# A seven-matmul prelude, exponentials on either of two engines, and wider staging in a fused attention, expert-attention and MLP kernel

## The chip, the cores and the metric

The kernel runs on one core of one Trainium2 chip. The metric is the device time of one execution in microseconds; a kernel's time is the median of several runs.

## What is computed

Three layers follow one another on data of 4 batches and 576 positions.

```
scores = 0.125 * q @ k.T          # 4 batches, 8 heads, 576 positions, width 64
# heads 0 to 3: key in the last 32 positions; heads 4 to 7: every 4th of the last 128
attn = softmax(where(mask, scores, -1e9)) @ v           # -> x, [4, 576, 512]
...
# 4 experts e, causal attention of width 64 each, the best 2 of 4 weighted per position
a = softmax(causal(0.125 * (x @ wq[e]) @ (x @ wk[e]).T))
x = sum over chosen e of w[e] * (a @ (x @ wv[e]) @ wo[e])
...
xn = (x - mean) / sqrt(var + 1e-6) * g_ln
out = x + relu(xn @ w_ch1) @ w_ch2                      # 512 -> 2048 -> 512
```

## The kernel before

**Stages.** Each batch goes through the windowed attention by pairs of heads (four pairs, written (b, hp); pairs 0 and 1 have the plain window, 2 and 3 the dilated one), then through projections for the experts, causal attention by tiles of 128 queries, and an output projection. All 2304 positions then go through the MLP, which is 1,824 wide matmuls and fills the time from about 320 us on. Products that need more than one pass of the fast number format are made of three matmuls of high and low parts.

**Order.** The order of the instructions on every engine is written by a planner in the kernel (`run_chains`). Each piece of work is a generator ("chain") that yields operations with an engine, an estimated duration and the times at which its inputs are ready. The planner always takes the operation that can start first, and so fixes each engine's program order from estimated times. An engine works through its own list strictly in that order: an instruction that waits holds up what stands behind it. Where a chain yields `either(...)`, the planner picks the engine that could start the operation first. The estimates are in `landing` (when a load is there), in `act` and `dve` (durations by elements) and in the numbers at each `op`.

**Loads.** All loads go through SyncE's queue (SP). `all_loads` lists them in a fixed order: per batch and pair q and k (`load_qk`), then v (`load_v`), with the weights in between. q and k land in two staging tiles, `nat`. A pair takes both, so the next pair's q and k can be issued when the transposes of the pair before have read them (`give("nat", t)`). In batch 0 pairs 1 and 2 use parts of `x2a` instead, a tile that holds the MLP's input later ("lent").

**Windows.** `turned_qk` transposes q and k on TensorE (PE, line 442, into the PSUM tile `ptr`) and copies them out as `qT` and `kT`. `scores` makes the scores of a pair in two PSUM banks (the mask is a matmul with the identity, then line 504). `window` runs once for each half of a pair, 32 times in all: the maximum by VectorE (DVE, line 525), the difference from PSUM to SBUF by DVE (527), the exponential by ScalarE (ACT, 530), the sum and the reciprocal by DVE (532, 534), the scaling by DVE or GpSimd (POOL, 536), the transposes on PE (548), and the product with v (565). A half has 5 or 4 blocks of 96 keys, or 6 blocks of 80.

**Expert attention.** `attend` works on 128 queries of two experts. The keys of tile i number 64, 192, 320, 448 or 576. A bank of PSUM holds 512 columns, so at 576 the scores are cut in two, `[(0, 64), (64, n)]`; each cut has one matmul with `KH` (778) and one with `KL` (779, the tile `klz`), and the last also one with the causal mask (781). Maxima and exponentials of the cuts are then joined (801 to 811). There are 16 such passes: 4 batches, 2 pairs of experts, 2 experts.

**Output projection.** `out_proj` writes the MLP's input into `x2a`, in batches 0 and 1 into the places 0 to 7.

Of the kernel before, what the change touches and what calls it, by code (L numbers as in the profile page):

```python
# [23 lines left out]
def windowed_attention_moe_mlp(  # L24
# [37 lines left out]
    QB = 8  # L62
    SCALE = 0.125
    DQ, DW = 48, 80
    NBD = S // DQ

    def qrange(i):
# [106 lines left out]
    def key(*k):  # L174
        return "key", k
# [28 lines left out]
    def run_chains():  # L204
        while chains:
            again = True
            while again:
                again = False
                for c in sorted(chains, key=lambda c: c[0]):
                    kind = c[2][0]  # L210
                    if kind == "acq" and len(places[c[2][1]]) >= c[2][2]:
                        tag, n = c[2][1:]
                        places[tag].sort()
                        at = places[tag][n - 1]
                        if tag == "bank":
                            taken.extend(x for _, x in places[tag][:n])
                            at = at[0]
                        del places[tag][:n]
                        resume(c, at)
                        again = True  # L220
                        break
                    if kind == "key" and c[2][1] in facts:
                        resume(c, facts[c[2][1]])
                        again = True
                        break
            best = None
            for c in chains:
                if c[2][0] != "op":
                    continue
                _, engines, deps, tile = c[2]  # L230
                for name, ns in engines:
                    engine = name.rstrip("*")
                    at = max([free[engine]] + [d + lag[engine] for d in deps])
                    if name != engine:
                        at = max(at, shared["POOL" if engine == "DVE" else "DVE"])
                    change = MODE if engine == "PE" and tile != mode[0] else 0.0
                    score = (at + change + (ns if len(engines) > 1 else 0.0) * 0.0, c[0])
                    if best is None or score < best[0]:
                        best = score, c, name, ns, at + change, tile
            assert best is not None, [(c[0], c[2]) for c in chains]  # L240
            _, c, name, ns, at, tile = best
            engine = name.rstrip("*")
            if name != engine:
                shared[engine] = at + ns + 80.0
            free[engine] = at + ns
            if engine == "PE":
                mode[0] = tile
            resume(c, (at + ns + tail[engine], engine) if len(c[2][1]) > 1 else at + ns + tail[engine])
# [72 lines left out]

    SLOT = (3, 2, 4, 1, 5, 0, 6, 7, 8)

    def landing(t, kb):

        land[0] = max(t + 600.0, land[0]) + 4.76 * kb
        return land[0] + 1200.0

    def issue(e, dst, src):
# [8 lines left out]
    def load_qk(b, hp, engines="SS"):  # L338
        h0 = 2 * hp
        cw = 8 if h0 >= H // 2 else 6  # L340
        pw = S // cw
        lent = b == 0 and hp in (1, 2)
        t = (yield acq("nat", 2)) if not lent else 0.0
        nats, times = [], []
        for x, src in enumerate((q, k)):
            if lent:
                nat = x2a[:, 4 * hp - 4 + 2 * x:4 * hp - 2 + 2 * x].rearrange("p a n -> p (a n)")
            else:
                nat = win.tile([P, 2 * DM], F32, tag="nat", name="nat", bufs=2)
            nat = nat[:pw, :cw * 2 * D].rearrange("p (c h d) -> p c h d", c=cw, h=2)  # L350
            e = "ACT" if engines[x] == "A" else "SP"
            ti = yield op(e, 780.0, [t])
            issue(e, nat, src[b, h0:h0 + 2].rearrange("h (p c) d -> p c h d", c=cw))
            nats.append(nat)
            times.append(landing(ti, 288.0))
        LD[b, hp] = nats, times
        put("ld", b, hp, at=0.0)

    def load_v(b, hp, engines=("SP",)):
# [39 lines left out]
        LV[b, hp] = vt, tv, home  # L399
        put("lv", b, hp, at=0.0)  # L400

    def all_loads():
        yield from room(0)
        yield from load_qk(0, 0)
        yield from load_qk(0, 1)
        yield from load_v(0, 0)
        yield from load_qk(0, 2)
        yield from load_v(0, 1)
        yield from load_qk(0, 3)
        yield from load_weights(0)  # L410
        yield from load_v(0, 2)
        yield from load_v(0, 3)
        yield from load_weights(1)
        yield from load_weights(2)
        for b in range(1, B):
            yield from room(b)
            for hp in range(NHP):
                yield from load_qk(b, hp)
                yield from load_v(b, hp)
                if b == 1 and hp == 1:  # L420
                    yield from load_weights(3)

    def turned_qk(b, hp):

        yield key("ld", b, hp)
        nats, times = LD[b, hp]
        tq = yield acq("qT")
        qT = win.tile([P, S], F32, tag="qT", name=f"qT{b}_{hp}", bufs=2)
        kT = win.tile([P, W + S], F32, tag="kT", name=f"kT{b}_{hp}", bufs=2)
        yield op("POOL", 130.0, [tq])  # L430
        nc.gpsimd.memset(kT[:, 0:W], 0.0)
        dil = 2 * hp >= H // 2
        cw = 8 if dil else 6
        pw, ch = S // cw, cw // 2
        ends = []
        for x in range(4):
            nat, hf = nats[x // 2], x % 2
            ta = yield acq("bank")
            pt = bank("ptr")
            t = yield op("PE", ch * turn(pw), [ta, times[x // 2]])  # L440
            for c in range(ch):
                nc.tensor.transpose(pt[:, pw * c:pw * (c + 1)],  # L442
                                    nat[:, hf * ch + c].rearrange("p h d -> p (h d)"), ident[:pw, :pw])
            if hf and not (b == 0 and hp in (1, 2)):
                give("nat", t)
            dst = kT[:, W:] if x > 1 else qT
            if dil:
                dst = dst.rearrange("p (c j x) -> p x c j", c=4, x=2)[:, hf]
                sp = pt[:, :HS].rearrange("p (c j) -> p c j", c=4)
            else:  # L450
                dst = dst.rearrange("p (j c) -> p j c", c=cw)[:, :, hf * ch:(hf + 1) * ch]
                sp = pt[:, :HS].rearrange("p (c j) -> p j c", c=ch)
            if x > 1:
                t, e = yield either(("ACT", 345.0), ("DVE", 366.0), deps=[t, tq])
                copy_by(e, dst, sp)
            else:
                t, e = yield either(("ACT", 345.0), ("DVE", 366.0), deps=[t, tq])
                if e == "ACT":
                    nc.scalar.mul(dst, sp, SCALE)
                else:  # L460
                    nc.vector.tensor_scalar(dst, sp, SCALE, None, op0=ALU.mult)
            give_bank(pt, t)
            ends.append(t)
        TQ[b, hp] = qT, kT
        put("qT", b, hp, at=max(ends))
# [44 lines left out]
    def window(b, hp, u):  # L510
# [11 lines left out]
        sc = sx[:, :nb, off:96]  # L522
        mx, sm, rs = [win.tile([P, NBD // NU], F32, tag=x, name=x, bufs=5)[:, :nb] for x in ("mx", "sm", "rs")]
        t = yield op("DVE", dve(kw * nb), [t])
        nc.vector.tensor_reduce(mx, psv, axis=AX.X, op=ALU.max)
        t = yield op("DVE", dve(kw * nb), [t, ts])
        nc.vector.tensor_tensor(sc, psv, mx[:, :, None].to_broadcast([P, nb, kw]), op=ALU.subtract)
        give_bank(ps, t)
        t = yield op("ACT", act(kw * nb, False), [t])
        nc.scalar.activation(sc, sc, AF.Exp)  # L530
        t = yield op("DVE", dve((kw + 1) * nb), [t])
        nc.vector.tensor_reduce(sm, sx[:, :nb, off:], axis=AX.X, op=ALU.add)
        t = yield op("DVE", 85.0, [t])
# [24 lines left out]
        vt, tv, home = LV[b, hp]  # L558
        ta = yield acq("bank")
        po = bank("po")  # L560
        t = yield op("PE", nb * (91.0 if dil else 114.0), ends + [ta, tv], "columns")
        for tt, t_ in enumerate(blk):
            for h in range(2):
                z = side(u, HALVES[h]).start // 64
# [187 lines left out]
    def attend(b, pr_, i):  # L752
# [16 lines left out]
        Pp = att.tile([P, 2, S], F32, tag="P", name="Pp", bufs=DB + 1)  # L769
        Ps, tsum = [], []  # L770
        for ee in range(2):
            cuts = [(0, n)] if n <= 512 else [(0, 64), (64, n)]
            tb = yield acq("bank", len(cuts))
            pss, tss = [bank("s2") for _ in cuts], []
            for (a, z), ps in zip(cuts, pss):
                end = z == n
                t = yield op("PE", 2 * max(0.4415 * (z - a) + 5.0, 90.0) + (55.0 if end else 0.0), [tb, tq])
                nc.tensor.matmul(ps[:m, :z - a], SQ[ee][:, q0:q0 + m], KH[ee][:, a:z], start=True, stop=False)  # L778
                nc.tensor.matmul(ps[:m, :z - a], SQ[ee][:, q0:q0 + m], KL[ee][:, a:z], start=False, stop=not end)  # L779
                if end:  # L780
# [125 lines left out]
    def out_proj(b, i):  # L906
# [10 lines left out]
        if ti >= NTA:  # L917

            yield key("fr", b, (ti - NTA) // 2)
        elif HOME[ti] >= LENT:  # L920
            for hp in range(NHP):
                t = max(t, (yield key("x", B - 1, hp)))
# [275 lines left out]

    with tc.manual_schedule():
        chain(-20.0, all_loads())  # L1200
        for b in range(B):
            for hp in range(NHP):
                chain(b * 10 - 7 - 5.3 + 0.5 * hp, turned_qk(b, hp))
# [64 lines left out]
```

## Time and profile before

| | us |
|---|---|
| median of 3 runs (lowest, highest) | 723.19 (722.45, 726.18) |
| the profiled execution, its time | 725.05 |
| its span, first to last instruction | 723.3 |
| TensorE busy in it | 700.0 |
| VectorE, ScalarE, GpSimd busy | 524.5, 287.0, 165.1 |

The span is what the trace covers; the execution's own time lies 1.75 us over it. Busy time counts an engine's instructions and leaves out its waits. TensorE's matmuls overlap: one is at work for longer than the distance to the next one's start, and it is this distance ("pitch") that a stream of them costs.

### The profile page before, as it was taken

The page shows a single profiled execution, that of the slowest core. Times are in us where ns is not written, and L with a number is a line of the kernel's source. Part 1 is how long each engine was busy: PE and PEld are TensorE (multiplying, and loading weights), DVE is VectorE, ACT ScalarE, POOL GpSimd, SP SyncE. Part 2 cuts the span into 40 slices and gives each one's busy share as a digit, 9 for nine tenths or more (in the row PEclk, how much of TensorE's full clock was granted, in tenths as well). Part 3 has the DMA queues.
Part 4 walks back from the last instruction along what each step waited for, and adds up shares of the span by engine and source line. Part 5 has one row for each costly group of instructions (what it writes and reads, how often), then busy time and mean ns, then how long its engine had stood idle before and what let it go on. Part 6 is the DMA issues. An engine that isn't in the chain of part 4 may idle for free.

```text
span 723.3 us, 13830 instructions
## 1 busy us (share of the span) xinstructions
PE 700.0 (97%) x5396; PEld 588.5 (81%) x5396; DVE 524.5 (73%) x1240; ACT 287.0 (40%) x754; POOL 165.1 (23%) x190
## 2 busy tenths in 40 slices
PE   6799999999999999999999999999999999999997
PEld 4788787988898888877878888888888888888886
DVE  4759879968989999994588874774774865844343
ACT  3566757656656667851242231220221211311100
POOL 3641113110011325220035351230330420410000
PEclk9999999999999999999999999999999999999999
DMA  9953541033312112000002121020110110100123
GB/s 166 200 134 83 115 102 46 18 67 74 82 42 69 38 47 68 30 30 1 1 29 88 59 87 30 30 86 2 59 58 1 61 56 12 47 1 1 58 88 116
DMA packets 78385, 43.10 MB, mean 60 GB/s; under 512 B 60145, under 2 KB 73713, under 8 KB 78321
## 3 DMA queue, kind: packets, MB, share of 16 engines
q1 hardware_dynamic: 78320, 42.23, 23.2%
q8 instruction: 42, 0.69, 0.4%
q14 instruction: 23, 0.18, 0.1%
HBM read 35.14 MB, written 4.72 MB: 55 GB/s over the span
## 4 chain that ended last, share of the span: by engine, by line
PE 84%; DVE 5%; DMA 4%; ACT 3%; SPq 2%; issue 1%; POOL 0%; ACTq 0%; DVEq 0%; POOLq 0%
PE phid L1157 28%; PE pout L1179 28%; PE pp L706 5%; PE pv L605 3%; PE pwo L929 3%; PE ppt L854 2%; DMA nat<-in_q_dram 2%; PE po L565 2%; PE ppt L548 2%; PE py L875 2%; SPq L330 2%; PE s L778 2%; PE s L779 2%; PE ptr L442 2%; PE py L873 1%; PE s L504 1%
## 5 line engine op out<-in xcount | busy, mean ns | idle before, releaser
L1179 PE MATMUL pout<-wp,ht 128*128 128x512 f32 x864 | 220.1, 395 | 0.0
L1157 PE MATMUL phid<-xn,wp 128*128 128x512 f32 (+1 forms) x960 | 218.9, 371 | 0.0
L1157 PEld LDWEIGHTS phid<-xn,wp 128*128 128x128 f32 x960 | 168.8, 188 | 34.4
L1179 PEld LDWEIGHTS pout<-wp,ht 128*128 128x128 f32 x864 | 160.0, 188 | 35.1 <-ACT ht L1162 0.2
L1162 ACT ACTIVATE ht<-phid 128x512 fp32r<-128x512 f32 (+1 forms) x80 | 44.4, 554 | 225.1 <-PE phid L1157 225.1
L1188 DVE SCALAR_TENSOR_TENSOR x2a<-pout,rstd,x2a 128x512 f32<-128x512 f32 x124 | 92.5, 748 | 53.9 <-PE pout L1179 53.1
L1164 DVE SCALAR_TENSOR_TENSOR ht<-phid,ht 128x512 fp32r<-128x512 f32 (+1 forms) x80 | 50.8, 635 | 58.6 <-ACT ht L1162 57.9
L1031 POOL TENSOR_TENSOR d_pw<-d_pw,d_t 128x512 f32<-128x512 f32 x32 | 41.6, 1299 | 184.9 <-DVE d_pw L1028 151.7
L1043 POOL TENSOR_TENSOR wp<-d_pw,wp 128x512 fp32r<-128x512 f32 x32 | 44.3, 1384 | 45.7 <-ACT wp L1041 45.7
L536 POOL TENSOR_TENSOR sc<-sc,rs 128x480 f32<-128x480 f32 (+1 forms) x24 | 22.9, 963 | 88.2 <-DVE rs L534 62.8
L251 ACT COPY pT<-ppt 80x288 f32<-80x288 f32 (+6 forms) x77 | 32.1, 426 | 19.5 <-PE ppt L854 9.9
L1015 ACT ACTIVATE d_sq<-ws 128x512 f32<-128x512 f32 x32 | 21.6, 676 | 44.0 <-DVE d_pw L1034 25.3
L794 ACT ACTIVATE Pp<-s,nm 128x448 f32<-128x448 f32 (+3 forms) x64 | 30.3, 476 | 12.5 <-DVE nm L792 11.5
L1041 ACT CAST wp<-d_pw 128x512 fp32r<-128x512 f32 x32 | 19.9, 621 | 35.6 <-DVE d_pw L1034 32.9
L778 PE MATMUL s<-KH,SQ 128*128 128x64 f32 (+4 forms) x96 | 32.6, 347 | 0.2
L1034 DVE SCALAR_TENSOR_TENSOR d_pw<-d_sq,d_pw 128x512 f32<-128x512 f32 x32 | 22.0, 689 | 14.7 <-POOL d_pw L1031 14.7
L442 PE MATMUL ptr<-ident,nat 72*128 72x72 f32 (+1 forms) x196 | 24.4, 246 | 7.2 <-DMA nat<-in_q_dram 6.4
L548 PE MATMUL ppt<-ident,sc 112*80 112x112 f32 (+1 forms) x168 | 27.2, 282 | 3.9 <-POOL sc L536 2.4
L779 PE MATMUL s<-klz,SQ 128*128 128x64 f32 (+4 forms) x96 | 30.2, 315 | 0.0
L1188 DVE SCALAR_TENSOR_TENSOR x2b<-pout,rstd,x2b 128x512 f32<-128x512 f32 x32 | 24.0, 749 | 8.4 <-PE pout L1179 8.2
L854 PE MATMUL ppt<-ident,Pp 128*128 128x128 f32 x160 | 28.5, 283 | 0.4 <-DVE yl L892 0.2
L792 DVE TENSOR_REDUCE nm<-s 128x1 f32<-128x448 f32 (+3 forms) x64 | 26.3, 415 | 3.1 <-PE s L781 2.3
(166 smaller groups left out, 1294.9 us busy)
## 6 DMA issues: line engine op xcount, KB each, us to landing
ws<-in_moe_w_ch_dram SPq DMA_DIRECT2D x32, 512.0 KB, 3.5
nat<-in_q_dram SPq DMA_DIRECT2D x14, 288.0 KB, 4.0
nat<-in_k_dram SPq DMA_DIRECT2D x14, 288.0 KB, 6.6
out_dram<-x2a SPq DMA_DIRECT2D x12, 256.0 KB, 2.0
KH<-KH SPq DMA_DIRECT2D x32, 72.0 KB, 1.9
vt<-in_v_dram SPq DMA_DIRECT2D x10, 192.0 KB, 3.9
x2a<-in_v_dram SPq DMA_DIRECT2D x8, 160.0 KB
vt<-in_v_dram SPq DMA_DIRECT2D x8, 160.0 KB
```

The source lines that it names most:

```text
L442: nc.tensor.transpose(pt[:, pw * c:pw * (c + 1)], nat[:, hf * ch + c].rearrange("p h d -> p (h d)"), ident[:pw, :pw])
L548: nc.tensor.transpose(pt[:kw, P * (tt - a):P * (tt - a) + pw], sc[:pw, tt], ident[:pw, :pw])
L778: nc.tensor.matmul(ps[:m, :z - a], SQ[ee][:, q0:q0 + m], KH[ee][:, a:z], start=True, stop=False)
L779: nc.tensor.matmul(ps[:m, :z - a], SQ[ee][:, q0:q0 + m], KL[ee][:, a:z], start=False, stop=not end)
L854: nc.tensor.transpose(pt[:, P * (j - 1):P * j], Ps[ee][:, k0:k0 + P], ident)
L1031: nc.gpsimd.tensor_tensor(pf, pf, t1.bitcast(F32), op=ALU.add)
L1043: nc.gpsimd.tensor_tensor(lo, pf, hi.bitcast(F32), op=ALU.subtract)
L1157: nc.tensor.matmul(ph[:, :n_tok], ws[:, c * P:(c + 1) * P], xs[c], start=n == 0, stop=n == 3 * KC - 1)
L1162: nc.scalar.activation(hh[:, :n_tok], ph[:, :n_tok], AF.Relu)
L1164: nc.vector.scalar_tensor_tensor(hl[:, :n_tok], ph[:, :n_tok], 0.0, hh[:, :n_tok].bitcast(F32), op0=ALU.max, op1=ALU.subtract)
L1179: nc.tensor.matmul(po, a_[:, sl], w_, start=n == 0, stop=n == 3 * len(fs) - 1)
L1188: nc.vector.scalar_tensor_tensor(x2(i), po, rstd[:, i:i + 1], x2(i), op0=ALU.mult, op1=ALU.add)
```

## The change

There are six edits.

1. A chain `warm` puts seven matmuls on PE ahead of everything else. Each multiplies the identity by the identity repeated four times (512 columns, bf16), into a PSUM bank that nobody reads. They need only `ident_bf`.
2. In `window` the maximum is taken negated. The subtraction and the exponential are then done either as before (DVE, then ACT), or by ACT alone: one exponential for each block straight from PSUM, with the negated maximum as its bias, 5, 4 or 6 instructions in place of one. The planner takes the engine that could start first; at the same time it takes DVE.
3. q and k of batch 1, pairs 1 and 2, land in the same parts of `x2a` as those of batch 0. Their loads wait for batch 0's transposes of the same pair (`key("nq", 0, hp)`), no longer for the `nat` tiles. `out_proj` into places 0 to 7 then waits for batch 1's transposes.
4. The 576 keys of the last tile are cut at 288, not at 64.
5. The planner's estimate of a load is 5.4 ns per KB, not 4.76, and a load now also makes SP busy in the planner up to 3.2 us before its landing.
6. Three of the planner's estimates for PE are raised: 25 ns more for each group of q and k transposes, 110 for 91 ns in the dilated product with v, 100 for 55 ns for the last cut's mask.

Edits 5 and 6, and the engines picked in edit 2, change no operation by themselves, but the order that the planner writes for the whole kernel.

```diff
-    def landing(t, kb):
-
-        land[0] = max(t + 600.0, land[0]) + 4.76 * kb
+    def landing(t, kb, e="SP"):
+
+        land[0] = max(t + 600.0, land[0]) + 5.4 * kb
+        free[e] = max(free[e], land[0] - 3200.0)
         return land[0] + 1200.0
...
-        lent = b == 0 and hp in (1, 2)
-        t = (yield acq("nat", 2)) if not lent else 0.0
+        lent = b < 2 and hp in (1, 2)
+        if not lent:
+            t = yield acq("nat", 2)
+        else:
+            t = (yield key("nq", 0, hp)) if b else 0.0
...
+    def warm():
+
+        t = yield acq("bank")
+        b = bank("warm")
+        t = yield op("PE", 2900.0, [t, 1750.0])
+        for _ in range(7):
+            nc.tensor.matmul(b.rearrange("p (x n) -> p x n", n=P), ident_bf,
+                             ident_bf[:, None].to_broadcast([P, 4, P]), start=True, stop=True)
+        give_bank(b, t)
...
-            t = yield op("PE", ch * turn(pw), [ta, times[x // 2]])
+            t = yield op("PE", ch * turn(pw) + 25.0, [ta, times[x // 2]])
...
-            if hf and not (b == 0 and hp in (1, 2)):
+            if hf and not (b < 2 and hp in (1, 2)):
                 give("nat", t)
+            if x == 3:
+                put("nq", b, hp, at=t)
...
-        nc.vector.tensor_reduce(mx, psv, axis=AX.X, op=ALU.max)
-        t = yield op("DVE", dve(kw * nb), [t, ts])
-        nc.vector.tensor_tensor(sc, psv, mx[:, :, None].to_broadcast([P, nb, kw]), op=ALU.subtract)
-        give_bank(ps, t)
-        t = yield op("ACT", act(kw * nb, False), [t])
-        nc.scalar.activation(sc, sc, AF.Exp)
+        nc.vector.tensor_reduce(mx, psv, axis=AX.X, op=ALU.max, negate=True)
+        t, e = yield either(("DVE", dve(kw * nb), 0.0), ("ACT", nb * 222.0, LEAN), deps=[t, ts])
+        if e == "DVE":
+            nc.vector.tensor_tensor(sc, psv, mx[:, :, None].to_broadcast([P, nb, kw]), op=ALU.add)
+            give_bank(ps, t)
+            t = yield op("ACT", act(kw * nb, False), [t])
+            nc.scalar.activation(sc, sc, AF.Exp)
+        else:
+            for tt in range(nb):
+                nc.scalar.activation(sc[:, tt], psv[:, tt], AF.Exp, bias=mx[:, tt:tt + 1])
+            give_bank(ps, t)
...
-        t = yield op("PE", nb * (91.0 if dil else 114.0), ends + [ta, tv], "columns")
+        t = yield op("PE", nb * (110.0 if dil else 114.0), ends + [ta, tv], "columns")
...
-            cuts = [(0, n)] if n <= 512 else [(0, 64), (64, n)]
+            cuts = [(0, n)] if n <= 512 else [(0, HS), (HS, n)]
...
-                t = yield op("PE", 2 * max(0.4415 * (z - a) + 5.0, 90.0) + (55.0 if end else 0.0), [tb, tq])
+                t = yield op("PE", 2 * max(0.4415 * (z - a) + 5.0, 90.0) + (100.0 if end else 0.0), [tb, tq])
...
+        elif ti < 8:
+            t = max(t, (yield key("nq", 1, 1 + ti // 4)))
...
         chain(-20.0, all_loads())
+        chain(-19.0, warm())
```

`LEAN` is 0.0, and `HS` is 288.

## Rows read from the trace of the kernel before

**Rows 1.** The page's first part: busy time, share of the span, instructions.
```profile
PE 700.0 (97%) x5396; PEld 588.5 (81%) x5396; DVE 524.5 (73%) x1240; ACT 287.0 (40%) x754; POOL 165.1 (23%) x190
```
**Rows 2.** Windows: stretch, length, each engine's busy time, granted clock, DMA share, GB/s.
```profile
5.00:12.40 7.40, 7.11 (x72) 5.69 (x72) 2.66 (x6) 2.01 (x5) 0.12 (x1) 1.00 1.23 189
12.40:24.00 11.60, 10.03 (x248) 8.28 (x242) 10.85 (x27) 7.62 (x19) 4.62 (x8) 1.00 1.07 177
24.00:30.00 6.00, 2.89 (x31) 2.31 (x32) 4.99 (x12) 2.63 (x7) 4.24 (x8) 0.96 1.08 227
30.00:42.00 12.00, 11.14 (x120) 10.39 (x118) 4.58 (x10) 7.03 (x18) 7.42 (x11) 0.88 0.73 131
42.00:82.00 40.00, 37.54 (x590) 34.42 (x589) 34.73 (x92) 26.10 (x73) 10.40 (x19) 1.00 0.52 119
82.00:88.00 6.00, 4.52 (x68) 3.76 (x64) 5.36 (x20) 3.72 (x12) 0.99 (x1) 0.72 0.73 149
88.00:320.00 232.00, 228.26 (x2423) 196.86 (x2419) 208.50 (x675) 152.75 (x466) 47.92 (x53) 1.00 0.22 54
320.00:700.00 380.00, 379.11 (x1774) 311.06 (x1773) 242.36 (x384) 81.92 (x154) 86.18 (x68) 1.00 0.13 41
```
**Rows 3.** Waits of PE: who for whom, us in total, times, longest.
```profile
PE ptr L442 <- DMA nat<-in_q_dram: 6.4, 3, 5.0
...
PE s L504 <- ACT kT L251: 1.5, 1, 1.5
...
PE ptr L442 <- DMA x2a<-in_k_dram: 0.6, 1, 0.6
```
**Rows 4.** Timeline of PE at the start: start, us, instruction.
```profile
5.01 1.20 PE L442 MATMUL ptr<-ident,nat 96*128 96x96 f32 x6 [5.01 <-DMA nat<-in_q_dram]
...
8.25 1.86 PE L504 MATMUL s<-kT,qT 64*64 64x96 f32 x36
...
12.77 1.04 PE L504 MATMUL s<-kT,qT 64*64 64x96 f32 x36
```
**Rows 5.** Timeline of PE: one pass over 576 keys, and what follows.
```profile
169.80 0.28 PE L778 MATMUL s<-KH,SQ 128*128 128x64 f32 x1
...
170.02 0.47 PE L778 MATMUL s<-KH,SQ 128*128 128x512 f32 x1
170.33 0.39 PE L779 MATMUL s<-klz,SQ 128*128 128x512 f32 x1
...
170.63 0.42 PE L442 MATMUL ptr<-ident,nat 96*128 96x96 f32 x3
```
**Rows 6.** Timeline of PE: projection matmuls of 288 columns.
```profile
68.31 0.38 PE L706 MATMUL pp<-xh,wqh 128*128 128x288 f32 x1
...
68.53 0.29 PE L706 MATMUL pp<-xl,wqh 128*128 128x288 f32 x1
...
68.65 0.29 PE L706 MATMUL pp<-xh,wql 128*128 128x288 f32 x1
```
**Rows 7.** Groups of DVE and ACT up to 320 us: count, busy us, mean ns.
```profile
L527 DVE TENSOR_TENSOR sc<-s,mx 128x480 f32<-128x480 f32 x24 | 15.3, 646 | 0.1
```
**Rows 8.** The same view of ACT.
```profile
L530 ACT ACTIVATE sc<-sc 128x480 f32<-128x480 f32 x24 | 14.2, 606 | 5.0 <-DVE sc L527 4.8
...
L794 ACT ACTIVATE Pp<-s,nm 128x320 f32<-128x320 f32 x16 | 8.5, 531 | 4.5 <-DVE nm L792 4.3
...
L794 ACT ACTIVATE Pp<-s,nm 128x64 f32<-128x64 f32 x16 | 5.0, 315 | 1.4 <-DVE nm L792 1.0
```
**Rows 9.** Timeline of ACT: an exponential from PSUM and its successor.
```profile
172.29 0.31 ACT L806 ACTIVATE Pp<-s,nm 128x64 f32<-128x64 f32 x1
172.51 0.19 ACT L806 ACTIVATION_READ_ACCUMULATOR Pp<-s,nm 128x1 f32 x1
```
**Rows 10.** Timeline of SP's queue: issues of q for batch 1, pairs 1 and 3.
```profile
39.55 0.59 SPq L330 DMA_DIRECT2D nat<-in_q_dram  x1
...
61.54 0.86 SPq L330 DMA_DIRECT2D nat<-in_q_dram  x1
```
**Rows 11.** Timeline at 82 us: ACT's queue ahead of the kT copies.
```profile
82.20 0.20 ACT L890 CAST yhs<-py 128x64 fp32r<-128x64 f32 x1
82.29 0.53 ACT L794 ACTIVATE Pp<-s,nm 128x320 f32<-128x320 f32 x1
...
82.80 0.78 ACT L251 COPY kT<-ptr 128x288 f32<-128x288 f32 x2
```

More of the change, by code (lines that the diff above doesn't have):

```diff
@@ L64, in windowed_attention_moe_mlp @@
     DQ, DW = 48, 80
+    LEAN = 0.0
     NBD = S // DQ
@@ L230, in run_chains @@
                 _, engines, deps, tile = c[2]
-                for name, ns in engines:
+                for name, ns, *lean in engines:
                     engine = name.rstrip("*")
@@ L236, in run_chains @@
                     change = MODE if engine == "PE" and tile != mode[0] else 0.0
-                    score = (at + change + (ns if len(engines) > 1 else 0.0) * 0.0, c[0])
+                    score = (at + change + sum(lean), c[0])
                     if best is None or score < best[0]:
```

## The prediction

> **What bounds the kernel now.** I begin with the busy shares: PE is at work for 97% of the span and no other engine for more than 73% [rows 1]. A change here must therefore shorten PE's own work or fill its 23 us of idle time. The table of windows says where that time lies, as length minus busy time of PE [rows 2]. From 320 us on nearly none is left, so the MLP can't move, and nothing in the change touches it. Before 320 us, after the first matmul at 5.01 us [rows 4], the gaps are 0.29, 1.57, 3.11, 0.86, 2.46, 1.48 and 3.74 us, 13.5 in sum. The 5.0 us ahead of the first matmul wait for the first load [rows 3] and stay; the rest is behind the last matmul.
>
> The second thing to see is PE's clock. It is granted at half, 1.2 for 2.4 GHz, in three places. Two stand in the clock column: 6.00 x 0.04 x 2 + 12.00 x 0.12 x 2 = 3.4 us at half rate around 30 us, and 6.00 x 0.28 x 2 = 3.4 us around 85 us, each behind a stretch in which PE idled for a quarter of the time or more [rows 2]. The third is the start, where the column reads 1.00. The durations say otherwise: the same 36 score matmuls take 1.86 us at 8.25 us and 1.04 at 12.77 [rows 4]. PE runs at half rate from 5.0 to about 12.4 us.
>
> The third view is that of PE's waits. Beside the first load, the named ones are small: 1.4 us for two later loads of q, 0.6 for a load of k in batch 0, 1.5 once for a copy of kT by ACT [rows 3].
>
> **Scores in halves (edit 4).** This is the only edit that changes PE's work in the full stretch. A pass over 576 keys now takes 0.83 us, from 169.80 to the next instruction at 170.63 [rows 5]: the two matmuls of 64 columns come every 0.11 us, though so short, and the first of 512 holds its successor back by 0.31 us. Afterwards there are four matmuls of 288 columns. Projection matmuls of that size follow each other at 0.12 us (68.53 to 68.65), and at 0.22 us behind the first of a run [rows 6]. So 0.22 + 3 x 0.13 + 0.07 for the mask is 0.68 us, and 16 passes give 16 x (0.83 - 0.68) = 2.4 us. Bounds: without the slow first, 0.59 us and a gain of 3.8; if each matmul of a pass cost 0.22, as none of them then had its weights in time, 0.95 us and a loss of 1.9. I take the middle, as the passes are runs of the same sort as the projections. DVE's and ACT's work on the two cuts stays about equal: the same 576 elements in two instructions each.
>
> **Prelude (edit 1).** Seven matmuls of 512 columns, at half rate 512 / 1.2 = 427 ns, make 3.0 us. They need an identity that DVE has ready at about 1.8 us, so they end near 4.9 us, in time that is empty now, and delay the first transposes by at most 0.2 us. What they can give back is the half rate from 5.0 to 12.4 us: 7.1 us of busy time [rows 2], at full rate 3.6 us. Before, full rate came 7.4 us after PE's first work; after the two later idle stretches it came after 3.4 us at half rate. Counted from 1.9 us, that puts the rise between 5.3 and 9.3 us, and the saving between all of 3.6 and (12.4 - 9.3) / 2 = 1.5 us of PE time. Not all of that reaches the end. At 15 us PE waits for k of pair 2 of batch 0, 0.6 us [rows 3]; the loads keep the DMA engines full until 24 us [rows 2], and an earlier PE makes that wait longer by what it gained. DVE, though, starts its chain of windows with the first scores and is then busy for 10.85 of 11.60 us [rows 2], so it keeps what the scores gain. I book 1.5 us, bounds 0 and 3.6.
>
> **Either engine (edit 2).** A half of a pair in 5 or 6 blocks now costs DVE 646 ns for the difference and ACT 606 for the exponential [rows 7, 8], 1.25 us in line. On ACT alone, one block from PSUM with a bias lies between the 315 ns for 64 columns and 531 for 320 [rows 8]: 0.84 ns a column, 342 for 96 and 328 for 80. An instruction's successor starts 0.09 us before its end (172.29 + 0.31 against 172.51, [rows 9]), so five blocks take 5 x 0.25 + 0.09 = 1.34 us and six 6 x 0.24 + 0.09 = 1.52. A moved half relieves DVE of 0.65 us, adds 0.7 to 0.9 to ACT, and is itself later by 0.1 to 0.3 us less one handover. The page "ScalarE: Activation LUTs" of the Trainium skill, section "What ACT_TABLE_LOAD costs", speaks against the edit a little more strongly: with a bias taken from SBUF it gives some 280 ns plus 0.833 per column, with about 93 of overlap, from which I estimate 1.43 us for five blocks of 96; by it a moved half costs ACT 0.8 us, and the sum stays as it is while ACT has room.
>
> ACT has room: from 42 to 82 us it works 26.1 of 40 us, DVE 34.7 [rows 2]. The planner prefers ACT where DVE has another instruction to start; with DVE at 87%, I expect 16 to 24 of the 32 halves to go over. This costs PE nothing, and gains only where PE waits for DVE's chain. That is the stretch from 24 to 30 us: PE idles 3.1 of 6 us, DVE works 5.0, and it is followed by 3.4 us at half rate, which costs 1.7 [rows 2]. I book 1.5 of these 4.8 us for this edit with the earlier start, bounds 0 and 4.8, since loads are as full there (share 1.08).
>
> **Staging (edit 3).** q for pair 1 of batch 1 is issued at 39.55 us and for pair 3 at 61.54 [rows 10], after the transposes of the pairs before. With other tiles for pairs 1 and 2, pair 1 is issued straight behind v of pair 0, some 5 us sooner, and pair 3 once pair 0 is transposed and the v loads ahead have room. The transfers go into a stretch with DMA shares of 0.73 and 0.52 [rows 2], so there is room. SP's list is strictly ordered: what stands behind, the copies of KH among it, is passed by no more loads than before. The gain is the wait for q in batch 1, up to 1.4 us [rows 3], and more choice for the planner in the 2.5 us of gaps from 42 to 82. I book 1.5, bounds 0 and 2.5. The wait added to `out_proj` ends with transposes from about 60 us, and its first work comes far later; I book nothing.
>
> **Estimates (edits 5, 6).** They rewrite the order everywhere. The stall at 82 us is one that an order made: kT's copies stand behind two other instructions on ACT [rows 11], PE idles 1.48 us and then pays 1.7 at half rate [rows 2]. Another order will hardly repeat that; an equal one may arise elsewhere. I book a gain of 1.5 for its going and a loss of 1.0 for new ones, bounds minus 3.2 and plus 4.
>
> **Sum.** -2.4 - 1.5 - 1.5 - 1.5 - 1.5 + 1.0 = -7.4 us. Against the profiled execution's 725.05 us this gives 717.7; that execution lies 1.9 us above the median of 723.19, against which it would be 715.8. I predict 716.5 us, between the two and nearer to the median.
>
> **Rivals.**
> *Loads and order take it back.* The start is bound by transfers, the new order has as many gaps as the old, and only the halves and a little of the start remain: 723.19 - 2.4 - 0.5 = 720.3, within 0.5%. For it: DMA shares over 1.0 up to 30 us, and the wait for k at 15 us. Against it: DVE at 94% between 12.4 and 24 us [rows 2], which an earlier start and a lighter chain do help. Chance 0.22.
> *Most gaps close.* Both falls of the clock go (3.4 us), the start gives 3, halves 3.8 and half the gaps 5: 723.19 - 15 = 708. For it: DVE is the busiest after PE in the gapped stretches. Against it: six small gaps never close together. Chance 0.10.
> *ACT becomes late.* It is the opposite side: PE waits for kT, xh or pT behind blocks of exponentials on ACT, as once at 82 us. Each such stall costs 1.5 us and, with the fall of the clock, 3.2. ACT's share in 42 to 82 us goes from 65% to 65 + 8 x 0.8 / 40 = 81% if 8 halves move there. Gains of 7 us are used up by more than two such stalls; by four the kernel is slower, 723.19 - 7.4 + 4 x 3.2 = 728.6. Four in 230 us against one now speaks against it; that ACT's load was never this high speaks for it. Chance 0.08.
>
> **How the numbers follow.** A difference under 0.5%, 3.6 us, can hardly be told from no change here; the three runs shown span that much. My forecast, 716.5 with its own range of 712 to 719.5, has 0.60. Faster by over 0.5% (under 719.6): 0.60 and 0.10, less a little of the forecast's upper edge, 0.69. Within 0.5%: the first rival with that edge, 0.23. Slower: 0.08. The range that leaves out 2 in 10, half of the large gain and all of the slow case with some of the edges, is 709.5 to 722.5.
>
> **What would show it.** Right: a pass over 576 keys of about 0.68 us; the first score matmuls in little more than 1.04 us; q of batch 1 issued by 36 us for pair 1; 16 or more halves with exponentials in blocks, 0.25 us apart; less idle time and no half rate around 30 and 85 us; 320 us to the end as before, only earlier. Wrong: half rate still at 12 us; the wait for k at 15 us grown by all of the gain; PE's waits for ACT above 4 us; the stages from 42 to 320 us with more than their 7.7 us of gaps.

## The result and the profile after

The changed kernel takes 714.03 us, median of 6 runs (713.58 to 715.23), against 723.52 us for the kernel before (median of 6). The ratio is 0.9866, with a 95% interval of 0.9846 to 0.9886. It is faster by 9.5 us, 1.3%; the forecast was 716.5, in a range of 709.5 to 722.5.

The first part of the page of the changed kernel answers to [rows 1]:

```profile
span 713.2 us, 13905 instructions
...
PE 696.9 (98%) x5403; PEld 587.0 (82%) x5403; DVE 512.4 (72%) x1214; ACT 299.4 (42%) x838; POOL 169.9 (24%) x198
```

PE's 696.9 us hold 3.2 of the prelude, so the kernel's own work on it went from 700.0 to 693.7. The table of windows shows where the rest went (columns as in [rows 2]; the row of the MLP lies 10 us sooner, from 310 us, as the MLP is reached sooner):

```profile
5.00:12.40 7.40, 5.24 (x109) 3.99 (x107) 4.48 (x11) 3.38 (x10) 0.12 (x1) 1.00 1.18 193
12.40:24.00 11.60, 10.50 (x154) 9.07 (x154) 7.90 (x19) 6.21 (x20) 3.88 (x6) 0.71 1.02 186
24.00:30.00 6.00, 4.45 (x105) 3.37 (x104) 5.87 (x15) 4.49 (x17) 4.27 (x6) 1.00 1.10 195
30.00:42.00 12.00, 11.58 (x159) 10.70 (x155) 3.82 (x8) 8.18 (x22) 8.89 (x17) 1.00 0.91 167
42.00:82.00 40.00, 37.91 (x546) 34.01 (x547) 35.28 (x100) 29.01 (x96) 13.61 (x20) 1.00 0.53 115
82.00:88.00 6.00, 5.80 (x85) 5.19 (x84) 5.84 (x20) 4.78 (x14) 1.39 (x4) 1.00 0.47 102
88.00:320.00 232.00, 229.85 (x2441) 200.83 (x2441) 203.19 (x659) 161.09 (x515) 50.50 (x56) 1.00 0.22 56
...
310.00:690.00 380.00, 379.10 (x1773) 310.98 (x1772) 241.68 (x382) 81.22 (x153) 84.04 (x66) 1.00 0.12 39
...
88.00:200.00 112.00, 111.79 (x1439) 101.20 (x1439) 95.39 (x323) 79.74 (x272) 20.55 (x29) 1.00 0.30 69
```

The spans differ by 10.1 us, and three terms make it up. PE's gaps between 5 and 320 us are 2.16, 1.10, 1.55, 0.42, 2.09, 0.20 and 2.15 us, 9.7 in sum after 13.5, so 3.8 us less [rows 2]. The half rate around 30 and 85 us is gone, but there is a new one in the second row: 11.6 x 0.29 x 2 = 6.7 us. Before, 7.1 + 3.4 + 3.4 = 13.9 us passed at half rate, so half of the 7.2 us of difference, 3.6, is gained. The passes over 576 keys give 3.0 (below). That is 10.4, an estimate from these rows.

The start, in PE's timeline, answers to [rows 4]:

```profile
1.84 3.17 PE L413 MATMUL warm<-ident_bf 128*128 128x512 bf16 x7 [1.84 <-DVE ident_bf L93]
4.79 0.75 PE L457 MATMUL ptr<-ident,nat 96*128 96x96 f32 x6
...
7.72 1.04 PE L521 MATMUL s<-kT,qT 64*64 64x96 f32 x36 [0.32 <-DVE kT L252]
...
13.28 0.47 PE L457 MATMUL ptr<-ident,x2a 72*128 72x72 f32 x4 [1.44 <-DMA x2a<-in_q_dram]
...
15.87 2.19 PE L587 MATMUL po<-pT,vt 96*64 96x64 f32 x36
...
24.33 0.69 PE L587 MATMUL po<-pT,vt 96*64 96x64 f32 x16
```

The same 36 matmuls (`po`) in the kernel before:

```profile
18.86 1.27 PE L565 MATMUL po<-pT,vt 96*64 96x64 f32 x36
```

The prelude ends in time, the first scores run at full rate, PE then waits 1.44 us for q of pair 2, and the 36 matmuls at 15.87 us take 2.19 us where the same work took 1.27 before: the clock has fallen again. This is one execution. The mean granted clock is 0.994 in two of the changed kernel's six runs, the profiled one among them, and 0.999 or 1.0 in the other four, so a fall of this length seems not to be the rule.

A pass over 576 keys in the same view answers to [rows 5]:

```profile
171.24 0.38 PE L800 MATMUL s<-KH,SQ 128*128 128x288 f32 x1
171.46 0.29 PE L801 MATMUL s<-klz,SQ 128*128 128x288 f32 x1
171.59 0.29 PE L800 MATMUL s<-KH,SQ 128*128 128x288 f32 x1
171.72 0.29 PE L801 MATMUL s<-klz,SQ 128*128 128x288 f32 x1
171.86 0.23 PE L803 MATMUL s<-mdiag,ident_bf 128*128 128x128 bf16 x1
171.93 0.28 PE L859 MATMUL ph<-ident,Ph 128*128 128x128 f32 x1
```

0.69 us to the next instruction. Over the passes that the trace holds complete, the mean went from 0.83 us to 0.645, and 16 times the difference is 3.0 us. ACT's timeline shows a half in blocks, and its table of groups all such halves of five or four blocks:

```profile
9.86 1.25 ACT L551 ACTIVATE sc<-s,mx 128x96 f32<-128x96 f32 x5
```
```profile
L551 ACT ACTIVATE sc<-s,mx 128x96 f32<-128x96 f32 x60 | 15.3, 360 | 5.8 <-DVE mx L542 5.7
```

The waits of PE that later readings compare with:

```profile
PE ptr L457 <- DMA x2a<-in_q_dram: 1.4, 1, 1.4
...
PE ppt L570 <- POOL sc L558: 1.0, 2, 0.8
...
PE ptr L457 <- DMA nat<-in_k_dram: 0.8, 1, 0.8
```

SP's timeline has the loads of q for pairs 1 and 3 of batch 1, as in [rows 10]:

```profile
35.41 0.59 SPq L332 DMA_DIRECT2D x2a<-in_q_dram  x1
...
61.24 0.86 SPq L332 DMA_DIRECT2D nat<-in_q_dram  x1
```

### The profile page after: what moved, and what is told of

Same layout as the page of the kernel before. It is cut to its first block, busy times and chain, and to the rows that moved or that the text cites. A ratio compares the mean times of both kernels' runs of the same rounds, so it can differ in the third digit from the quotient of the medians.

```text
span 713.2 us, 13905 instructions
## 1 busy us (share of the span) xinstructions
PE 696.9 (98%) x5403; PEld 587.0 (82%) x5403; DVE 512.4 (72%) x1214; ACT 299.4 (42%) x838; POOL 169.9 (24%) x198
## 4 chain that ended last, share of the span: by engine, by line
PE 82%; DVE 10%; ACT 4%; issue 2%; DMA 1%; POOL 1%; SPq 0%; DVEq 0%; ACTq 0%; POOLq 0%
PE pout L1203 28%; PE phid L1181 28%; PE pp L728 5%; PE pv L627 3%; PE pwo L953 3%; PE ppt L876 2%; PE po L587 2%; PE ptr L457 2%; PE py L897 2%; PE ppt L570 2%; PE s L521 1%; PE s L800 1%; PE s L801 1%; PE py L895 1%; ACT Pp L816 1%
## 5 line engine op out<-in xcount | busy, mean ns | idle before, releaser
L1067 POOL TENSOR_TENSOR wp<-d_pw,wp 128x512 fp32r<-128x512 f32 x32 | 42.8, 1339 | 43.2 <-ACT wp L1065 43.2
L558 POOL TENSOR_TENSOR sc<-sc,rs 128x480 f32<-128x480 f32 (+1 forms) x28 | 26.8, 966 | 63.2 <-DVE rs L556 20.2
L252 ACT COPY pT<-ppt 80x288 f32<-80x288 f32 (+7 forms) x76 | 33.0, 447 | 14.1 <-PE ppt L876 10.0
L816 ACT ACTIVATE Pp<-s,nm 128x64 f32<-128x64 f32 (+3 forms) x64 | 30.6, 479 | 13.0 <-DVE nm L814 10.9
L800 PE MATMUL s<-KH,SQ 128*128 128x288 f32 (+4 forms) x96 | 31.2, 330 | 0.1
L551 ACT ACTIVATE sc<-s,mx 128x96 f32<-128x96 f32 (+1 forms) x108 | 26.6, 353 | 11.2 <-DVE mx L542 10.8
L1045 DVE SCALAR_TENSOR_TENSOR d_t<-ws,d_t 128x512 int32<-128x512 int32 x32 | 28.7, 896 | 0.4
L801 PE MATMUL s<-klz,SQ 128*128 128x288 f32 (+4 forms) x96 | 28.5, 302 | 0.0
L814 DVE TENSOR_REDUCE nm<-s 128x1 f32<-128x64 f32 (+3 forms) x64 | 25.7, 415 | 3.4 <-PE s L803 2.9
```

What stands on the lines that cost most here:

```text
L816: nc.scalar.activation(Pt[:m, :n], pss[0][:m, :n], AF.Exp, bias=nm[:m, ee:ee + 1], accum_out=sm[:m, ee:ee + 1])
L1067: nc.gpsimd.tensor_tensor(lo, pf, hi.bitcast(F32), op=ALU.subtract)
```

## The experiments

All ratios are to the kernel before, timed beside each kernel on the same chip; their intervals are some 0.2% wide to either side, 1.5 us. Differences of 1 to 2 us between two of these kernels are therefore not told apart. Differences in us are of medians, to 714.03 us of the changed kernel or 723.52 of the one before, across three series on three chips; by the ratios they come out between 0.5 us smaller and 1.4 us larger. Four of the kernels keep the changed kernel's order of instructions on every engine and alter only the operation in question ("order held"); in the others the planner writes a new order. Where the order is held, a matmul can be looked up in both profiles, and the difference of its two start times says where time is won or lost.

**Without the prelude, order held.**

```diff
-        for _ in range(7):
+        for _ in range(0):
             nc.tensor.matmul(b.rearrange("p (x n) -> p x n", n=P), ident_bf,
```

> The changed kernel without its seven prelude matmuls; the planner still reckons with them, so the order of every other instruction on every engine is that of the changed kernel. Theory (the prelude is worth the half rate that it removes): PE runs at half rate from 4.8 to about 12 us again, the first 36 score matmuls take 1.8 us and not 1.04, and the time rises by 2 to 3.5 us, to 716 to 717.5. Rival (the gain is given back by the wait for q of pair 2 at 13.3 us and by the fall of the clock from 15.2 to 22.0 us that comes after it): the scores end 2 us later, the wait of 1.44 us shrinks to under 0.3, the half rate at 15 us doesn't occur, and the time stays within 1 us of 714.0.

Measured: 714.96 us, ratio 0.9881 (0.9859 to 0.9902). That is the rival: 0.9 us above the changed kernel, inside the noise. PE's timeline of this kernel:

```profile
8.63 1.86 PE L521 MATMUL s<-kT,qT 64*64 64x96 f32 x36
...
15.52 0.53 PE L570 MATMUL ppt<-ident,sc 128*96 128x128 f32 x3 [1.25 <-POOL sc L558]
...
23.36 0.69 PE L587 MATMUL po<-pT,vt 96*64 96x64 f32 x16
```

The first scores run at half rate and end 1.7 us later (10.49 against 8.76). Yet the 16 matmuls for pair 1 start at 23.36 us, and in the changed kernel's profiled execution, which fell back to half rate, at 24.33; from there to the MLP this kernel stays ahead of that execution, by 0.5 us at 320 us. The expectation of a shorter wait for q held too: it is gone, but a new one of 1.25 us for POOL's scaling stands in nearly the same place.

**Cut at 64, order held.** The cut is `(0, 64), (64, n)` again, and the planner's estimates are those of the cut at 288.

> The changed kernel with the cut of the last tile's keys at 64 again, while the planner reckons with the cut at 288, so the order is that of the changed kernel. Theory (PE's own work): the pass goes from a mean of 0.645 us to 0.83, 16 passes cost 2.9 us, and the time rises to about 717. Rival (passes wait for DVE or banks anyway, so their length is hidden): under 1 us, 714 to 715.

Measured: 716.47 us, ratio 0.9913 (0.9886 to 0.994). 2.4 us slower than the changed kernel; the trace's 15 complete passes have a mean of 0.79 us. PE's matmuls start 1.5 us sooner than in the changed kernel's profile at 90 us, and 1.0 later at 320, so some 2.5 us are lost in the stretch of the passes. The theory holds, a little smaller.

**The subtraction on DVE, order held.**

```diff
-        if e == "DVE":
+        if True:
             nc.vector.tensor_tensor(sc, psv, mx[:, :, None].to_broadcast([P, nb, kw]), op=ALU.add)
             give_bank(ps, t)
-            t = yield op("ACT", act(kw * nb, False), [t])
+            if e == "DVE":
+                t = yield op("ACT", act(kw * nb, False), [t])
             nc.scalar.activation(sc, sc, AF.Exp)
```

> The changed kernel with the difference on DVE and one exponential on ACT in all 32 halves, put at the very places where the changed kernel has its blocks of exponentials; no other instruction moves on any engine. DVE gets 21 more instructions of 0.65 us, ACT loses 16 us or so. Theory (relief of DVE closes PE's gaps): PE's idle time up to 320 us grows from 9.7 us by 2 to 5 us, most of it ahead of 60 us, and the time rises to 716 to 719. Rival (the order closed the gaps, DVE has room): within 1 us of 714.0.

Measured: 723.79 us, ratio 1.0001 (0.9986 to 1.0016): the whole gain is gone, 9.8 us, more than the theory asked for. Windows, and PE's waits between 88 and 200 us:

```profile
42.00:82.00 40.00, 36.90 (x523) 32.51 (x523) 34.09 (x96) 23.93 (x69) 11.47 (x16) 0.96 0.47 101
...
88.00:200.00 112.00, 108.21 (x1369) 96.19 (x1370) 97.88 (x321) 70.21 (x218) 20.92 (x33) 1.00 0.31 71
```
```profile
PE ppt L877 <- ACT qT L476: 1.2, 1, 1.2
PE ptr L457 <- ACT qT L476: 0.7, 1, 0.7
```

PE's gaps grow by 1.0 us from 42 to 82 and by 3.6 from 88 to 200 us, where the changed kernel has 0.2; not ahead of 60 us, as I had expected. The start times agree: from 26 to 50 us PE's matmuls are level with the changed kernel's profile, at 82 us 3.1 us later (up to 1.6 of it by half rate, 40.00 x 0.04 x 2 = 3.2 us), and from 220 us on 8.4. The two largest waits between 88 and 200 us are for ACT's copies of qT, though ACT has less work in this kernel (70.2 us of 112 after 79.7): it looks held up, not overloaded. But this order was written for blocks on ACT, so part of the 9.8 us may be the order's unfitness, and the replanned kernel is the fairer test.

**The subtraction on DVE, replanned.** `either` gets DVE alone.

> The changed kernel without the choice of ACT; the planner knows it and writes its order for it. Theory (relief of DVE): 716 to 718, a little better than with the order held, as the planner avoids the worst waits. Rival (the order alone): 713 to 715, as any order of the new planner is about as good.

Measured: 721.63 us, ratio 0.9966 (0.9947 to 0.9985), 7.6 us slower than the changed kernel and beyond the theory's 716 to 718. Replanning saved only 2 us. The twelve runs spread from 718.43 to 724.16 us, and the profile is of the fastest. Its windows and its largest wait of PE:

```profile
42.00:82.00 40.00, 34.83 (x525) 30.81 (x527) 35.14 (x94) 25.41 (x74) 9.29 (x15) 1.00 0.54 119
```
```profile
PE ppt L570 <- POOL sc L558: 4.8, 5, 1.8
```

PE idles 5.2 us from 42 to 82 us (2.1 in the changed kernel), and 4.8 us of its waits in all are for the scaled scores, the last step of a window, which the changed kernel awaits for 1.0 us.

**Staging as before, replanned.** `lent` is `b == 0 and hp in (1, 2)` again.

> The changed kernel with q and k of batch 1 in the two staging tiles again; the planner writes its order for it. Theory (edit 2 carries most of the gain, staging little): q for pair 1 of batch 1 is issued at about 40 us again, PE idles up to 1.5 us more from 42 to 82 us, 714.5 to 716. Rival (staging gave the planner the choice that closes the gaps): 717 or more, with PE's idle time up to 100 us back at its old height.

Measured: 715.42 us, ratio 0.9897 (0.9883 to 0.9911). 1.4 us slower, as the theory had it, and at the edge of what can be told. The place is not the one expected: PE idles 2.2 us from 42 to 82 us, where the changed kernel idles 2.1, and 4.5 after 2.2 from 88 to 320.

**The planner's old estimates, replanned.** 4.76 ns per KB, no hold on SP, and the three old numbers for PE.

> The changed kernel with the planner's old estimates (edits 5 and 6 undone), all operations as in the changed one but for the engine that the planner picks. Theory (relief of DVE makes the gain under either set of estimates): 713 to 716. Rival (better estimates make a better order, the operations little): 718 or more.

Measured: 718.8 us, ratio 0.9946 (0.9932 to 0.996). That is the rival's bound: 4.8 us slower, with 21 halves on ACT all the same. PE's waits, and a window:

```profile
PE ptr L456 <- DMA nat<-in_q_dram: 2.3, 3, 0.8
...
PE ptr L456 <- DMA x2a<-in_q_dram: 1.6, 2, 1.1
...
PE ptr L456 <- DMA x2a<-in_k_dram: 1.1, 1, 1.1
```
```profile
24.00:42.00 18.00, 14.47 (x165) 13.22 (x158) 8.05 (x18) 9.62 (x30) 11.06 (x17) 0.72 0.99 180
```

PE waits 5.0 us for q and k, where the changed kernel waits 2.2 (1.4 for q and 0.8 for k). The likely reason is that with loads reckoned too fast transposes stand too early in PE's list, and what is ready stands behind them. From 24 to 42 us the clock is at half for 18 x 0.28 x 2 = 10.1 us, where the changed kernel's rows show full rate.

**Matmuls of the identity in the wait as well, order held.**

```diff
+    def filler():
+
+        yield key("s1", 0, 1)
+        t = yield acq("bank")
+        b = bank("warm")
+        t = yield op("PE", 0.0, [t])
+        for _ in range(7):
+            nc.tensor.matmul(b.rearrange("p (x n) -> p x n", n=P), ident_bf,
+                             ident_bf[:, None].to_broadcast([P, 4, P]), start=True, stop=True)
+        give_bank(b, t)
```

> The changed kernel with seven more matmuls of the identity by itself, put where PE waits for q of pair 2 (behind the scores of pair 1, at about 11.8 to 13.3 us); nothing else moves on any engine. At full rate they take 1.5 us, the length of that wait; at half rate 3.0. Theory (an early rise is given back by the fall that follows the wait): where full rate comes early the half rate from 15 to 22 us doesn't occur and the time falls by 1 to 2 us, to 712 to 713; where it comes only at 10 us nothing is gained and up to 1 us lost. Rival (the start is set by loads and by DVE, whatever PE's rate is): 714.0 within 1 us.

Measured: 714.57 us, ratio 0.9892 (0.9875 to 0.9908): the rival. PE's timeline, a window of it, and its waits from 24 to 42 us:

```profile
11.68 1.68 PE L425 MATMUL warm<-ident_bf 128*128 128x512 bf16 x7
...
21.59 0.69 PE L599 MATMUL po<-pT,vt 96*64 96x64 f32 x16
```
```profile
24.00:42.00 18.00, 14.88 (x206) 0.91 0.95 190
```
```profile
PE ppt L582 <- POOL sc L570: 2.7, 3, 1.8
```

The half rate at 15 us doesn't occur, and PE starts the product of pair 1 at 21.59 us, 2.7 sooner than in the changed kernel's profile. Then it idles 3.1 us from 24 to 42 us (2.0 there), 2.7 of them for POOL's scaling, and falls to half rate in that stretch. The matmuls that the changed kernel's profile has from 24 to 30 us start 2.7 us sooner here, and those that it has from 38 us on 0.7 later: what is gained at the start is lost by then.

**All halves on ACT, replanned.** `either` gets ACT alone.

> The changed kernel with exponentials in blocks on ACT in all 32 halves, not in 21; the planner knows it. DVE loses another 11 x 0.65 = 7 us of work, ACT gains some 8. Theory (DVE is the limit in PE's gaps, each moved half is worth 7.6 / 21 = 0.36 us): 11 more halves bring up to 4 us, 710 to 712. Rival (the two engines were in balance, ACT is late now): 714 to 719, with waits of PE for ACT where those for DVE stood.

Measured: 720.89 us, ratio 0.9969 (0.9957 to 0.9982), 6.9 us slower: the sign is the rival's, the size is beyond its 714 to 719. A stretch of ACT and POOL, and a window:

```profile
24.80 2.73 ACT L551 ACTIVATE sc<-s,mx 128x80 f32<-128x80 f32 x12 [1.05 <-DVE mx L542]
27.34 0.49 ACT L301 CAST wvh<-ws_att 128x260 fp32r<-128x260 f32 x1
...
27.91 0.75 POOL L303 TENSOR_TENSOR wvl<-ws_att,wvh 128x260 fp32r<-128x260 f32 x1 [1.00 <-ACT wvh L301]
```
```profile
24.00:42.00 18.00, 15.57 (x148) 13.89 (x149) 6.74 (x17) 9.07 (x30) 12.14 (x19) 0.72 0.98 177
```

Twelve blocks stand ahead of a cast of weights, and POOL waits 1.00 us for it. But PE's longest waits are for POOL's scaling (3.0 us in four), not for ACT as the rival had it, and from 24 to 42 us the clock is at half for 10.1 us here too. The relief of DVE has no fixed price per half; that ACT's blocks alone are the cause is not shown, since the order is another one.

**The estimates alone.** The kernel before with edits 5 and 6.

> The kernel before with the planner's new estimates alone (edits 5 and 6); all operations are those of the kernel before. Theory (the estimates are worth what their undoing cost, 4.8 us, whatever else is there): 718 to 720. Rival (they only help together with the choice of an engine, or the 4.8 us were the luck of one order): 721 to 725.

Measured: 717.14 us, ratio 0.9896 (0.9871 to 0.9921). Without one changed operation the kernel is 6.4 us faster than before, more than the theory had. Its waits of PE:

```profile
PE ptr L443 <- DMA nat<-in_q_dram: 5.9, 2, 4.7
PE ppt L549 <- POOL sc L537: 4.9, 5, 2.5
...
PE ptr L443 <- DMA x2a<-in_q_dram: 0.4, 1, 0.4
...
PE ptr L443 <- DMA nat<-in_k_dram: 0.3, 1, 0.3
```

Behind the first load (4.7 us) PE waits 1.9 us for q and k, and 2.2 in the kernel before. So shorter waits for loads are not what this kernel gains by. Its gaps are smaller from 24 to 30 us (1.1 after 3.1) and from 82 to 320 (1.6 after 5.2), and larger from 12.4 to 24 (2.3 after 1.6) and from 42 to 82 us (4.5 after 2.5).

**The choice of an engine alone.** The kernel before with edit 2.

> The kernel before with the choice of an engine alone (edit 2); the planner puts 23 of 32 halves on ACT. Theory (relief of DVE carries the gain): 716 to 718, since its undoing cost 7.6 us. Rival (half of those 7.6 us needs the new estimates): 719 to 722.

Measured: 720.56 us, ratio 0.9956 (0.9937 to 0.9974): the rival, 3.0 us faster than before.

**Two other orders of the same operations.** `dve(n)` with 66.0 for 65.0, and `MODE` with 126.0 for 128.0.

> The changed kernel with the planner's fixed share of a DVE instruction at 66 ns and not 65. No operation changes; the planner writes another order, with some 45% of PE's list in other places, and picks ACT for 22 halves, not 21. It shows what the luck of an order is worth. Theory (replanned variants are good to about 1.5 us): 712.5 to 715.5. Rival (the order alone moves the time by as much as the edits do): more than 3 us away from 714.0.

> The changed kernel with the planner's price for a change of PE's tiling at 126 ns and not 128: another order of the same operations, 22 halves on ACT. Theory: 712.5 to 715.5. Rival: more than 3 us away from 714.0.

Measured: 714.7 us, ratio 0.9869 (0.9847 to 0.9891), and 717.19 us, ratio 0.9906 (0.9884 to 0.9929). One order is as good as the changed kernel's, as the theory had it; the other is 3.2 us worse, at the rival's bound.

No kernel that was run is faster than the changed one.

## Why the prediction came out, and where its terms were off

**Bound and place.** PE is the bound, the MLP kept its time, and all of the gain lies ahead of 320 us, in gaps, half rate and PE's own work, as the prediction laid it out.

**Halves.** 2.4 us booked; 2.4 in the time of the kernel with the order held and 2.5 by PE's start times there, 3.0 by the lengths of the passes. The slow first matmul of a pass (0.22 us, then 0.13) is there as read from [rows 6].

**Prelude.** 1.5 us booked, bounds 0 and 3.6; 0.9 measured, not told from nothing. The rival's mechanism, given back, is what the profiled executions show; the wait behind it is for q of pair 2 and not for k. Two things hide a gain: POOL's and the loads' part in the stretch from 24 to 42 us, and a clock that doesn't always follow (last section). The four runs of the changed kernel at 0.999 or 1.0 have a median of 713.6 us, 1.3 below the kernel without the prelude; so few runs don't settle whether the 1.5 is there when no fall follows.

**Either engine.** 1.5 us booked, bounds 0 and 4.8. The step that failed is the one that let the relief pay only from 24 to 30 us. Alone the edit gains 3.0 us, its undoing costs 7.6 replanned and 9.8 with the order held, and the added time lies later: from 50 to 220 us with the order held; replanned, PE's gaps grow from 42 to 82 us (5.2 after 2.1) and from 200 to 320 (3.6 after 1.9). What is late there are the steps of a window behind DVE's, ACT's copies and POOL's scaling among them. The prediction's list of waits [rows 3] left out the largest one behind the first load, which is for that scaling (`sc`):

```profile
PE ppt L548 <- POOL sc L536: 2.4, 5, 0.8
```

The changed kernel waits 1.0 us there, and the two kernels with the new estimates and no blocks on ACT wait 4.8 and 4.9. But the slower of the two other orders, with blocks, waits as long (2.3 us for POOL and 2.6 for the scalings that DVE does), so an order alone can make this wait. The numbers of halves (21, expected 16 to 24) and the length of five blocks were right in kind, but a block follows the one before at 0.22 us and not 0.25: five take 1.25 us where 1.34 were read from [rows 8, 9]. The estimate of 1.43 us from the page "ScalarE: Activation LUTs" of the Trainium skill (section "What ACT_TABLE_LOAD costs") is further off; its 360 ns for a single one of 96 columns agrees with the mean of the changed kernel's 60, 360 ns, and its overlap of 93 ns doesn't, as the trace has 138 (360 less 222, the pitch of the five in 1.25 us).

**Staging.** 1.5 us booked, 1.4 measured. q of pair 1 came 4 us sooner (35.41), as said; q of pair 3 hardly did (61.24 after 61.54), since v of pair 2 stands ahead of it in SP's list and is issued at 59.91 us, after a wait of 8.6 us for a product of PE (`po`). That the gain is the wait for q, as booked, is not shown.

**Estimates.** A gain of 1.5 and a loss of 1.0 booked, 0.5 net, bounds minus 3.2 and plus 4; 4.8 us by undoing them and 6.4 by making them alone, both beyond the bounds. The prediction took them for a reshuffling around one stall. The new rate of a load is nearer to the trace up to 24 us: 189 and 177 GB/s [rows 2] are 5.4 and 5.8 ns for a KB of 1024 bytes, where the old estimate was 4.76. Undone, they lengthen PE's waits for loads by 2.8 us. But made alone they shorten these waits by 0.3 us only, so why that order is 6.4 us better stays open, and so does which of edits 5 and 6 does it.

**ACT late.** The rival of the other side did not come in the changed kernel. With 32 halves in place of 21 the kernel is 6.9 us slower, but with half rate and waits for POOL, not with the stalls for ACT that the rival names.

**Half rate elsewhere.** The prediction counted two falls of the clock and booked their going once. They weigh in the other orders as well: the mean granted clock is 0.985 to 0.994 in all eighteen runs with the old estimates or with all halves on ACT. At their middle values, 0.991 and 0.9915, PE spends 2 x 0.009 x 717 = 12.9 and 2 x 0.0085 x 719 = 12.2 us at half rate, where the changed kernel at 0.999 spends 1.4. Half of the difference, 5.7 and 5.4 us, is an upper estimate of what this costs, beside 4.8 and 6.9 us lost. It does not explain every loss: the slower of the two other orders ran at 1.0 in four of six runs.

**The sum** of 7.4 us came near 9.5 because the passes were right and terms too small for edits 2, 5 and 6 met a start that gave less than booked. That it came so near is in part luck: another order of the same operations moves the time by up to 3.2 us, more than the 2.1 us by which the sum was off, and the edits don't add up. Undoing them one by one costs 0.9 + 2.4 + 7.6 + 1.4 + 4.8 = 17.1 us of a gain of 9.5.

**What stays open** is how the gain divides between edit 2 and edits 5 and 6. The estimates alone give 717.1 us; the same with prelude, halves and staging, but without ACT's blocks, 721.6, though of these three the halves gain 2.4 us with the order held and the other two lose nothing where they were tested. So the order that the planner happens to write is worth 4.5 us in that pair, some 7 with the halves' gain, and up to 3 us between orders of the same operations. That is as much as the 7.6 us of edit 2 replanned, or the 4.8 and 6.4 of edits 5 and 6. Only the differences with the order held are free of it, and that of edit 2 has the reservation made there, that the order was written for the blocks. That the wait for POOL's scaling in the replanned kernel without blocks is due to DVE alone was not tried.

## What to carry to other kernels

Where a planner writes the order, test an edit with the order held, and run one or two neutral changes of an estimate to learn what the luck of an order is worth, before believing a few microseconds. Look at the waits for loads when a planner reckons them too fast: undoing the better estimates made them 2.8 us longer here. Look at the granted clock of every run, too, and not of the profiled one alone. Moving work between two engines need not pay in proportion: here 21 of 32 halves gained, and the kernel with all 32 lost 6.9 of the 9.5 us.

## What was not expected of the hardware

The clock doesn't follow the prelude in every execution. In ten profiled executions of kernels with the prelude, all starting at 1.83 or 1.84 us, the first 36 score matmuls took 1.04 us in seven and 1.86 to 1.87 in three (the cut at 64 and both kernels with the subtraction on DVE). In the four without it they took 1.81 to 1.86. Two kernels whose lists are alike up to there, the changed one and the one with the cut at 64, differ in it:

```profile
4.80 1.17 PE L457 MATMUL ptr<-ident,nat 96*128 96x96 f32 x6
...
8.07 1.86 PE L521 MATMUL s<-kT,qT 64*64 64x96 f32 x36
```

This is the kernel with the cut at 64; the changed one has 0.75 and 1.04 us for the same two rows. And the changed kernel, with the early rise, fell to half rate at 15.2 us for 6.8 us, while this one kept full rate from 10.4 us to the MLP's end. Either way the total time is the same within a few microseconds.
